# Output projection over 448 instead of 512 rows, with the moved rows placed by DMAs of GpSimd, and two chunks of layer 0 transposed by DMA instead of TensorE

## The chip, the cores and the metric

The kernel runs on one core of a Trainium2 chip. The metric is the device time of one execution in microseconds (us); of several executions the median is taken. Engines are named as the profile names them: PE is TensorE's matmul, PEld its weight load, DVE VectorE, ACT ScalarE, POOL GpSimd, SP the sync engine, whose queue issues most DMAs.

## The reference, cut to what matters

Four layers, alternately A and B, on x of 2048 tokens by 448 values in bfloat16. Layers 0 and 2 are A, layers 1 and 3 are B; both A layers share their weights, and so do both B layers.

```python
def _A_ref(x, wqkv, wo):            # H = 16 heads, Dh = 28, W, dil = 8, 2
    qkv = (x @ wqkv).reshape(B, S, 3, H, Dh).transpose(2, 0, 3, 1, 4)
    q, k, v = qkv[0], qkv[1], qkv[2]
    idx = pos[:, None] - (jnp.arange(W) * dil)[None, :]     # each token: 8 keys, every second one back
    logits = einsum("bhsd,bhswd->bhsw", q, k[idx]) * Dh ** -0.5   # masked where idx < 0
    o = einsum("bhsw,bhswd->bhsd", softmax(logits), v[idx])
    return o.transpose(0, 2, 1, 3).reshape(B, S, D) @ wo    # the output projection
def _B_ref(x, w_gate, w_up, w_down):                        # F = 1792
    return ((x @ w_gate) * (x @ w_up)) @ w_down
x = x + _A_ref(_layernorm(x), A_wqkv, A_wo)
x = x + _B_ref(_layernorm(x), B_w_gate, B_w_up, B_w_down)
x = x + _A_ref(_layernorm(x), A_wqkv, A_wo)
x = x + _B_ref(_layernorm(x), B_w_gate, B_w_up, B_w_down)
```

## The kernel before

**Tokens and layout.** Tokens are reordered: even ones first, odd ones after, so that a key "two back" is a neighbour. They form 16 blocks of 128 tokens. x_sb holds all of x, tokens on partitions. Two neighbouring blocks are a pair; there are 8 pairs in a layer.

**Jobs.** Each layer is cut into chunks of tokens (constants ACH and BCH): layers 0, 1 and 3 into 256, 512, 512, 512 and 256, layer 2 into four of 512. A job is one chunk of one layer. The list SEQ names them in the order in which they are handed to the planner, "A00 A01 B10 A02 ..."; the letter says A or B, then layer and chunk.

**An A job.** ln_chunk normalises each block (bn_stats and bn_aggr on DVE, L630 and L632; logarithm and exponential on ACT, L633 and L635; the product xn_sb on DVE, L651). The normalised block is transposed, to have the features on partitions. That is done by DMA from the sync queue (L654) or, for the chunks in PE_T, by four TensorE transposes (L660) with an eviction by ACT or DVE (L666). In the kernel before, PE_T holds all five chunks of layer 0; layer 2 and the B layers use the DMA. qk_chunk multiplies with the query and key weights (matmuls recorded at L698, evicted at L750), v_group with the value weights (L698, L842). Four of the sixteen heads' values take another way: written to DRAM by the sync queue (vt, L759) and read back by DMA transposes (L770); in layer 0 that holds only from query group 7 on. attn_front computes scores (L862), their exponential (L869) and the mask (L879). attn_back multiplies with the values (L896) and adds (L910, L914).

**Normalisation and projection.** Queries come in groups of 120 tokens (the first has 128), so a pair's columns come from three or four groups. norm spreads the softmax sum over a head's rows (L924), takes its reciprocal through logarithm and exponential (L925, L926), and multiplies into oT (L937, DVE). oT holds the attention output, features on partitions, as [128, 4, 1024]: four chunks c of four heads, each head 28 rows and 4 padding rows, so 4 x 128 = 512 rows of which 448 hold data; 1024 columns of tokens are used as a ring. y_blocks multiplies it with wo_g, the projection weights laid out in the same way with zeros in the padding rows (memset at L529). twin_blocks (matmul at L714) does this for the two blocks of a pair at once: each matmul takes 64 rows, and the upper and lower half of the array work at the same time, in part "flip 0" on one block each, in "flip 1" on the other. Over four chunks that makes 2 parts x 4 chunks x 2 halves = 16 matmuls for a pair. x_block adds the result to x_sb (L954).

**A B job.** b_chunk has 14 units of 14 matmuls for gate and up (L983), a copy by ACT (g_sb, L989), the product on DVE (hT, L992) and the down product (L714 again, or L1004 at the very end), then x_block. In layer 3 the result is stored.

**What sets the order.** The whole program is a list of operations with an estimated duration, dependencies and a priority (lower goes first). Sched.schedule runs through them in its own time and picks for each engine, whenever that is free, the most urgent operation that is ready; what comes out is each engine's fixed order. Priorities are a job's place in SEQ plus the tables JP (by job) and PR (by kind of operation) and HEAD_P for layer 0's normalisation. On PE, gated-product work has mode "R64" (MAIN), and the HOLD constants say when work of other modes goes ahead of it. Sched.emit then writes each engine's instructions in that order, with semaphore waits[...]. The estimates do not run on the chip, they only shape the order.

**Loads.** x is loaded by SP, the first four blocks as two halves; the query and key weights land in stage and are copied into the padded layout WQK by DVE and ACT (L573), with further columns filled in later (L581, by POOL and DVE). wo_g is filled by four DMAs of SP (L500); WD and WGU follow; then one DMA writes the ones into vt.

Of the kernel before, what the change touches and what calls it, by code (L numbers as in the profile page):

```python
# [7 lines left out]
ALU = mybir.AluOpType  # L8
# [20 lines left out]
PE_T = ("00", "01", "02", "03", "04")  # L29
HEAD_LN = 5  # L30
HEAD_P = (-53.71, -30.23, -20.33, -12.94, -19.33)
HOLD_A = 1000.0
HOLD_BA = 2000.0
HOLD_BB = 500.0
HOLD_N = 2
S_EST = 270.0
VX = 120.0
# [3 lines left out]
POOL_WQK = True  # L41
# [10 lines left out]
PR = {'AV': 8.84, 'rstd': -5.66, 'bn': 0.73, 'N': -2.82, 'Gps': -1.08, 'Tps': 16.85, 'H': 18.16, 'S': 10.61, 'VT': 19.61, 'Ex': 16.77, 'G': -2.93, 'xn': -6.19, 'QK': -6.56, 'Ddps': -26.52, 'V': 22.93, 'x': -0.84, 'lnv': -15.5, 'Oc': -6.51, 'Oa': -6.47, 'R': -19.3, 'VVps': 1.22, 'Yps': -25.3, 'PW': 58.69, 'T': -9.57, 'mv': 2.02, 'Rs': -2.57, 'Rl': 21.52, 'QKps': 4.71, 'E': -7.15, 'wqk': -9.31, 'wqp': -11.53}  # L52
JP = {'A20': -3.02, 'B32': 16.28, 'B34': 16.21, 'A22': 20.13, 'B13': 2.73, 'A21': 6.27, 'B12': -2.81, 'A02': -0.21, 'A03': 4.03, 'B30': 4.3, 'B31': 8.23, 'B10': 21.86, 'B11': -14.15, 'A23': 29.86, 'A04': -0.79, 'B33': 153.62, 'A01': -5.33, 'B14': 4.53, 'A00': -24.6}
XL = (2300.0, 2200.0, 4200.0, 5000.0, 5500.0)
WVL = 5000.0
STL = (2400.0, 2600.0, 2900.0, 2800.0)
VONES_L = 18000.0
# [8 lines left out]
SEED = 190  # L66
JITTER = 0
ATT_P = 1.96
# [61 lines left out]
class Sched:  # L130
# [9 lines left out]
    HICCUP = 210.0  # L140

# [5 lines left out]
    def add(self, engs, ins, est, deps=(), prio=0.0, mode=None, acquire=None, release=(), dma=None, lat=0.0, after=None, selfd=(), tmin=None):  # L147
# [8 lines left out]
        for _, k in ins:  # L156
            k = k[0] if isinstance(k, list) and k else k
            if isinstance(k, tuple) and k[0] in PR and k[0] != "cross":
                op.prio += PR[k[0]]
                break  # L160
# [57 lines left out]
    def schedule(self):  # L218
# [6 lines left out]
        credit, clast = self.CREDIT, 0.0  # L225
        ndep, users = {}, {}
# [20 lines left out]
        while left:  # L247
            moved = False
            b_ready = any(o.acquire is not None and o.acquire.kind == 1 for o in pend["pe"])
            for e in self.ENGS:  # L250
# [64 lines left out]
                if e == "pe":  # L315
# [7 lines left out]
                    credit = max(0.0, credit + est / self.FETCH - n)  # L323
                    clast = now + est
# [114 lines left out]
def build(nc, A_x, A_wqkv, A_wo, B_w_gate, B_w_up, B_w_down, out):  # L439
# [24 lines left out]
    wo_g = sb([128, 4, D], bf, "wo_g")  # L464
# [9 lines left out]
    oT = sb([128, 4, HALF], bf, "oT")  # L474
# [11 lines left out]
    sem_names += ["d_x0h"]  # L486
    sem_names += [f"d_t{li}_{j}" for li in range(4) for j in range(len(CH[li]))]
    sem_names += [f"d_p{li}_{j}" for li in (0, 2) for j in range(len(CH[li]))] + [f"d_v{q}" for q in range(NQB)] + ["d_one", "d_stv"]
# [10 lines left out]
    def plain_dma(q, dst, src, key, sem, deps=(), lat=3000.0, prio=0.0, tmin=None):  # L499
# [419 lines left out]
    def norm(li, g, qb, os_, prio):  # L919
# [8 lines left out]
        for B in range(tok // 128, (tok + nq - 1) // 128 + 1):  # L928
            if B >= 8:
                war.append(("Y", li, B - 8))  # L930
            elif li >= 2:
                war.append(("Y", li - 2, B + 8))
# [202 lines left out]
```

## Time and profile before

| | |
|---|---|
| median of 8 runs | 393.54 us (392.35 to 394.4) |
| the profiled execution's own time | 394.22 us |
| its span, from first to last instruction | 392.5 us |
| granted TensorE clock | 1.00 |
| output projection (L714 on wo_g, oT) | 256 matmuls, 349 ns mean of one |
| TensorE transposes (L660) | 64, on layer 0's 16 blocks |
| DMA transposes into xnTa (layer 2) and xnTb (layers 1, 3) | 16 and 32 |
| POOL, busy in all | 7.7 us |

A row of a group gives the line, engine, operation and tiles, then busy time and the mean of one. Matmuls overlap, so a matmul's mean is longer than the spacing of two. A row of a timeline gives start, length, engine and line, and in brackets the idle time before it and what ended it. A row of the table by stage gives the stretch, its length, and each engine's busy time and count, then the clock, the share of the DMA engines and GB/s.

### The profile page before, as it was taken

What the parts mean: (1) busy time and instruction counts of PE and PEld (TensorE: products, weight loads), DVE (VectorE), ACT (ScalarE), POOL (GpSimd) and SP (SyncE); (2) the same over time, 40 slices, a digit from 0 to 9 for tenths busy, and PEclk for the clock granted to TensorE, in tenths of its full rate; (3) what the DMA queues carried; (4) which work ended last, traced back from release to release, by engine and by line L of the source; (5) the groups of instructions that cost most, each with busy time, mean ns of one, the idle gap of its engine ahead of it and who ended that gap; (6) DMA issues with size and microseconds to landing.
All of it is one profiled execution on the core that took longest, in us unless ns stands there. A gap on an engine that the chain in (4) does not pass through costs nothing.

```text
span 392.5 us, 13910 instructions
## 1 busy us (share of the span) xinstructions
PE 384.7 (98%) x6142; PEld 213.8 (54%) x6142; DVE 271.2 (69%) x596; ACT 207.2 (53%) x398; POOL 7.7 (2%) x36
## 2 busy tenths in 40 slices
PE   8989999899999999999999999999999999999997
PEld 6645657545445544554546867444454544544674
DVE  6989899669966865684788645258942689377252
ACT  4888886478523744467651524268315782263230
POOL 6010000000000000000000000000000000000000
PEclk9999999999999999999999999999999999999999
DMA  8990161501220301310120241010050102502101
GB/s 278 294 302 20 24 93 29 107 10 30 48 48 15 78 18 25 69 35 15 17 48 16 42 95 29 25 20 11 8 124 14 26 7 47 97 3 16 34 27 47
DMA packets 54703, 22.47 MB, mean 57 GB/s; under 512 B 44836, under 2 KB 54644, under 8 KB 54644
## 3 DMA queue, kind: packets, MB, share of 16 engines
q1 hardware_dynamic: 53284, 19.47, 23.3%
q10 hardware_dynamic: 1360, 2.12, 1.9%
q8 instruction: 48, 0.79, 0.8%
q14 instruction: 11, 0.09, 0.1%
HBM read 8.54 MB, written 2.71 MB: 29 GB/s over the span
## 4 chain that ended last, share of the span: by engine, by line
PE 91%; DVE 3%; DMA 2%; ACT 2%; issue 1%; DVEq 0%
PE ps L983 41%; PE ps L714 25%; PE ps L698 17%; PE ps L896 3%; PE ps L862 3%; PE ps L1004 1%; DMA xnTb<-xn_sb 1%; PE ps L660 1%; DMA x_sb<-in_A_x_dram 1%; DVE st L630 1%; DVE xn_sb L651 1%; ACT R_sb L925 1%; ACT R_sb L926 1%; DVE x_sb L954 0%; PE ps L565 0%
## 5 line engine op out<-in xcount | busy, mean ns | idle before, releaser
L983 PE MATMUL ps<-xnTb,WGU 64*128 64x512 bf16 (+1 forms) x1960 | 180.5, 333 | 1.0 <-DMA xnTb<-xn_sb 1.0
L983 PEld LDWEIGHTS ps<-xnTb,WGU 64*128 64x128 bf16 x1960 | 93.6, 94 | 73.8 <-ACT g_sb L989 1.5
L989 ACT ACTIVATE g_sb<-ps 128x512 bf16<-128x512 f32 (+1 forms) x140 | 71.4, 510 | 95.2 <-PE ps L983 94.5
L992 DVE TENSOR_TENSOR hT<-g_sb,ps 128x512 bf16<-128x512 bf16 (+1 forms) x140 | 79.4, 575 | 55.3 <-ACT g_sb L989 45.5
L714 PE MATMUL ps<-WD,hT 64*128 64x448 bf16 x840 | 84.0, 349 | 0.1
L714 PEld LDWEIGHTS ps<-WD,hT 64*128 64x128 bf16 x840 | 40.2, 94 | 37.0 <-DVE hT L992 0.7
L698 PE MATMUL ps<-xnTa,WQK 64*128 64x512 bf16 (+1 forms) x504 | 53.5, 353 | 0.2
L954 DVE TENSOR_TENSOR x_sb<-x_sb,ps 128x448 bf16<-128x448 bf16 x62 | 36.2, 615 | 24.9 <-PE ps L714 24.8
L630 DVE BATCH_NORM_STATS2 st<-x_sb 128x6 f32<-128x448 bf16 x64 | 37.5, 617 | 2.5 <-DMA x_sb<-in_A_x_dram 2.5
L869 ACT ACTIVATE E_sb<-ps 128x1024 bf16<-128x1024 f32 (+1 forms) x36 | 33.5, 980 | 10.1 <-PE ps L862 9.5
L750 ACT ACTIVATE qk<-ps 128x1024 bf16<-128x1024 f32 (+1 forms) x30 | 27.1, 921 | 19.3 <-PE ps L698 19.0
L651 DVE TENSOR_SCALAR xn_sb<-x_sb,mv,rstd 128x512 bf16<-128x512 bf16 (+1 forms) x64 | 33.7, 571 | 4.6 <-ACT rstd L635 4.4
L698 PEld LDWEIGHTS ps<-xnTa,WQK 64*128 64x128 bf16 x504 | 23.5, 94 | 23.9 <-ACT xnTa L666 0.8
L879 DVE TENSOR_TENSOR E_sb<-E_sb,MK 128x1024 bf16<-128x1024 bf16 (+2 forms) x40 | 23.9, 613 | 9.2 <-ACT E_sb L869 9.0
L714 PE MATMUL ps<-wo_g,oT 64*128 64x448 bf16 x256 | 29.1, 349 | 0.0
L633 ACT ACTIVATE lnv<-mv,eps_sb 128x2 f32<-128x2 f32 (+1 forms) x33 | 9.5, 293 | 30.3 <-DVE mv L632 30.0
L937 DVE TENSOR_TENSOR oT<-O_sb,R_sb 128x480 bf16<-128x480 f32 (+3 forms) x36 | 22.1, 628 | 3.4 <-ACT R_sb L926 3.1
L925 ACT ACTIVATE R_sb<-R_sb 128x480 f32<-128x480 f32 (+1 forms) x34 | 20.1, 600 | 5.5 <-DVE R_sb L924 5.5
L924 DVE STREAM_SHUFFLE R_sb<-O_sb 128x480 f32<-128x480 f32 (+1 forms) x34 | 22.7, 695 | 0.0
L698 PE MATMUL ps<-WV,xnTa 64*128 64x336 bf16 (+3 forms) x252 | 22.3, 304 | 0.2
L926 ACT ACTIVATE R_sb<-R_sb 128x480 f32<-128x480 f32 (+1 forms) x34 | 20.1, 601 | 0.4
L714 PEld LDWEIGHTS ps<-wo_g,oT 64*128 64x128 bf16 x256 | 12.3, 94 | 11.6 <-DVE oT L937 0.4
(47 smaller groups left out, 170.7 us busy)
## 6 DMA issues: line engine op xcount, KB each, us to landing
out_dram<-x_sb SPq DMA_DIRECT2D x15, 112.0 KB, 1.7
WD<-in_B_w_down_dram SPq DMA_DIRECT2D x2, 784.0 KB, 11.3
WGU<-in_B_w_up_dram SPq DMA_DIRECT2D x2, 784.0 KB, 17.4
WGU<-in_B_w_gate_dram ACTq DMA_DIRECT2D x2, 784.0 KB, 14.1
x_sb<-in_A_x_dram SPq DMA_DIRECT2D x3, 448.0 KB, 6.2
vt<-qk SPq DMA_DIRECT2D x42, 16.0 KB
xnTb<-xn_sb SPq DMA_TRANSPOSE x32, 3.0
x_sb<-in_A_x_dram SPq DMA_DIRECT2D x2, 224.0 KB, 4.0
```

What stands on the lines that cost most here:

```text
L630: sc.add("dve", one(lambda E, B=B: E.bn_stats(st6[:, B, :], x_sb[:, B, :]), ("bn", li, B)), 525.0, deps=[("x", li - 1, B)] + ([("xn", li - ...
L651: sc.add("dve", one(lambda E, B=B, dst=dst, src=src: E.tensor_scalar(dst, src, mv[:, B, 0:1], rstd[:, B:B + 1], ALU.subtract, ALU.mult), ( ...
L698: parts[0 if s < 3 else 1][1].append((lambda E, w=w, c=c, lo=lo, st=st, sp_=sp_: E.matmul(u["out"](w), u["lhs"](w, c, lo, lo + 64), u["rhs ...
L714: ins.append((lambda E, w=w, c=c, lo=lo, st=st, sp_=sp_: E.matmul(outs(w), lhs(w, c, lo), rhs(w, c, lo), start=st, stop=sp_), keys[w] if s ...
L750: return E.activation(dst, src, ACT.Copy) if hasattr(E, "activation") else E.tensor_copy(dst, src)
L869: return E.activation(E_sb[:, slot, 2 * hp:2 * hp + 2, 0:w], ps[:, b0:b0 + 2, 0:w], ACT.Exp, scale=SCALE)
L925: sc.add("act", one(lambda E: E.activation(R_sb[:, rs, 0:w], R_sb[:, rs, 0:w], ACT.Ln), ("Rl", li, qb)), act_est(w, False), deps=[("Rs", l ...
L926: sc.add("act", one(lambda E: E.activation(R_sb[:, rs, 0:w], R_sb[:, rs, 0:w], ACT.Exp, scale=-1.0), ("R", li, qb)), act_est(w, False), de ...
L954: sc.add("dve", one(lambda E: E.tensor_tensor(x_sb[:, B, :], x_sb[:, B, :], ps[:, bk[w], 0:D], ALU.add), ("x", li, B)), dve_est(D), deps=[ ...
L983: ins.append((lambda E, u=u, k=k, w=w: E.matmul(u["out"](w), WGU[64 * w:64 * w + 64, k, 128 * u["fc"]:128 * u["fc"] + 128], X[64 * w:64 * ...
L989: sc.add("act", one(lambda E, gs=gs, bk=bk: E.activation(g_sb[:, gs, 0:nt], ps[:, bk[0], 0:nt], ACT.Copy), ("G", li, j, fc)), act_est(nt), ...
L992: sc.add("dve", one(lambda E, gs=gs, bk=bk, fc=fc: E.tensor_tensor(hT[:, fc, hs, 0:nt], g_sb[:, gs, 0:nt], ps[:, bk[1], 0:nt], ALU.mult), ...
```

## The change

**Projection.** 448 rows are seven halves of 64. For block w = 0 of a pair, the upper half of chunk 3 (heads 14 and 15, 56 rows) is copied into padding rows of the other chunks; for w = 1, the lower half (heads 12 and 13). MOVES lists four copies for each block, of 16, 16, 12 and 12 rows by 128 columns. They are DMAs from oT to oT, issued by POOL in y_blocks after all normalisations that the pair needs. Part flip 0 runs over four chunks as before, flip 1 over three, 14 matmuls for a pair. Both wait for all eight moves. The weights are kept twice, once for each block, with the rows moved in the same way: 16 DMAs of SP in place of four, without the memset, with a later place in SP's order (WO_P). oT becomes a ring of 768 columns, three pairs, that runs on through both A layers.

**Transposes.** Chunks 3 and 4 of layer 0 leave PE_T, so their six blocks are transposed by DMA from SP.

**The rest.** Copies of WQK are assigned by a list, three to ACT and five to DVE, and ACT's also wait for a layer-norm value. The first two blocks of x are loaded by one DMA each, the second by ACT's queue. A gate and up unit waits only for the half of the weights that it reads, and these units keep their order among themselves. The planner gets other priorities, other hold times, other estimates, and a model of instruction fetching on PE (the FL constants, not shown); PR, SEED, ATT_P and STL change too (not shown). SEQ, the number of matmuls in every other product and the tiling stay.

```diff
-PE_T = ("00", "01", "02", "03", "04")
+PE_T = ("00", "01", "02")
...
-HEAD_P = (-53.71, -30.23, -20.33, -12.94, -19.33)
+HEAD_P = (-20.43, -34.51, -10.86, -27.2, -5.58)
...
-POOL_WQK = True
+WQK_ACT = ((0, 0), (0, 1), (2, 0))
...
-JP = {'A20': -3.02, 'B32': 16.28, 'B34': 16.21, 'A22': 20.13, 'B13': 2.73, 'A21': 6.27, 'B12': -2.81, 'A02': -0.21, 'A03': 4.03, 'B30': 4.3, 'B31': 8.23, 'B10': 21.86, 'B11': -14.15, 'A23': 29.86, 'A04': -0.79, 'B33': 153.62, 'A01': -5.33, 'B14': 4.53, 'A00': -24.6}
+JP = {'A23': -110.04, 'B11': -19.53, 'B31': -48.16, 'A21': 10.97, 'A22': -168.43, 'B10': -33.38, 'A00': -17.62, 'B13': -8.8, 'B33': 6.0, 'A04': 7.36, 'A02': 0.78, 'A20': -111.99, 'B30': 1.74, 'B32': 5.39, 'A03': 25.81, 'B34': -31.77, 'A01': -6.89, 'B14': -32.55, 'B12': 1.5}
...
+STL = (2900.0, 3100.0, 3300.0, 3300.0)
+VONES_L = 15000.0
+MVL = 2400.0
+OW = 768
+WO_P = -43.2
+MVE = 1000.0
...
-    wo_g = sb([128, 4, D], bf, "wo_g")
+    wo_g = sb([128, 2, 4, D], bf, "wo_g")
...
-    oT = sb([128, 4, HALF], bf, "oT")
+    oT = sb([128, 4, OW], bf, "oT")
...
+        on_act = (q, lo) == (0, 1)
+        plain_dma("act" if on_act else "sp", x_sb[:, 4 * q + lo:4 * q + hi, :], x_par[two][:, b0 + lo:b0 + hi, :], [("x", -1, B) for B in range(4 * q + lo, 4 * q + hi)],
+                  f"d_x{q}" + "h" * lo, lat=XL[q + (q > 0 or lo > 1)], prio=-62 if on_act else -50 + q + 0.01 * lo)
+
+    load_x(0, 0, 1)
+    load_x(0, 1, 2)
     load_x(0, 2, 4)
...
-    memset("dve", wo_g[:], 0.0, "c_wo", 1000)
...
-            sc.add(("act", "dve", "pool") if POOL_WQK else ("act", "dve"), one(fn, ("wqk", c, w)), {"act": 470.0, "dve": 330.0, "pool": 600.0}, deps=[("stg", c), "c_wqk0"], prio=-28)
+            on_act = (c, w) in WQK_ACT
+            sc.add("act" if on_act else "dve", one(fn, ("wqk", c, w)), 560.0 if on_act else 300.0,
+                   deps=[("stg", c), "c_wqk0"] + ([("rstd", 0, int(WQK_ACT.index((c, w)) >= 1))] if on_act else []), prio=-28)
...
-    plain_dma("sp", ones_dst, ones_src, ("vones",), "d_one", deps=["c_ones"], lat=VONES_L, prio=-40)
-    for j in range(4):
-        dst = wo_g[32 * j:32 * j + DH, :, :]
-        src = A_wo.rearrange("(c j e) d -> j e c d", c=4, j=4, e=DH)[j]
-        plain_dma("sp", dst, src, ("wo", j), "d_wo", deps=["c_wo"], lat=WOL, prio=-45)
+    plain_dma("sp", ones_dst, ones_src, ("vones",), "d_one", deps=["c_ones"], lat=3000.0, est=VONES_L, prio=-40)
+    MOVES = ((0, 0, 64, 16), (0, 32, 96, 16), (0, 64, 80, 12), (0, 96, 112, 12), (1, 64, 0, 16), (1, 96, 32, 16), (1, 0, 16, 12), (1, 32, 48, 12))
+    for j in range(8):
+        src = A_wo.rearrange("(c j e) d -> j e c d", c=4, j=4, e=DH)[j % 4]
+        plain_dma("sp", wo_g[32 * (j % 4):32 * (j % 4) + DH, j // 4, :, :], src, ("wo", j), "d_wo", lat=WOL, prio=WO_P)
+    for n, (w, q, p, k) in enumerate(MOVES):
+        r0 = DH * (12 + p // 32) + p % 32
+        plain_dma("sp", wo_g[q + DH:q + 32, w, 0:k // 4, :], A_wo[r0:r0 + k, :].rearrange("(r c) d -> r c d", r=4), ("wo", 8 + n), "d_wo", lat=WOL, prio=WO_P)
...
-    WO = [("wo", j) for j in range(4)]
+    WO = [("wo", j) for j in range(16)]
...
-        for B in range(tok // 128, (tok + nq - 1) // 128 + 1):
-            if B >= 8:
-                war.append(("Y", li, B - 8))
-            elif li >= 2:
-                war.append(("Y", li - 2, B + 8))
-        cut = [tok] + [HALF] * (tok < HALF < tok + nq) + [tok + nq]
+        g0 = S * (li // 2)
+        for p in range(tok // 256, (tok + nq - 1) // 256 + 1):
+            q = p + 8 * (li // 2) - OW // 256
+            if q >= 0:
+                war += [("Y", 2 * (q // 8), 2 * (q % 8)), ("Y", 2 * (q // 8), 2 * (q % 8) + 1)]
+        cut = [tok] + [t - g0 for t in range(0, 2 * S, OW) if tok < t - g0 < tok + nq] + [tok + nq]
...
-                return E.tensor_tensor(oT[:, :, a % HALF:a % HALF + z - a], O[:, :, a - tok:z - tok], R_sb[:, rs, 0:w].rearrange("p (h n) -> p h n", h=4)[:, :, a - tok:z - tok], ALU.mult)
+                m = (a + g0) % OW
+                return E.tensor_tensor(oT[:, :, m:m + z - a], O[:, :, a - tok:z - tok], R_sb[:, rs, 0:w].rearrange("p (h n) -> p h n", h=4)[:, :, a - tok:z - tok], ALU.mult)
...
-        twin_blocks(lambda w: ps[:, bk[w], 0:D], lambda w, c, lo: oT[lo:lo + 64, c, 128 * ((B + w) % 8):128 * ((B + w) % 8) + 128], lambda w, c, lo: wo_g[lo:lo + 64, c, :],
-                    (("Y", li, B), ("Y", li, B + 1)), [range(4)], [[]], nd + WO, prio, bk)
+        p, m0 = B // 2, (128 * B + S * (li // 2)) % OW
+        for n, (w, q, p0, k) in enumerate(MOVES):
+            dst = oT[q + DH:q + 32, 0:k // 4, m0 + 128 * w:m0 + 128 * w + 128]
+            src = oT[p0:p0 + k, 3, m0 + 128 * w:m0 + 128 * w + 128].unsqueeze(1)
+            sc.add("pool", one(lambda E, dst=dst, src=src: E.dma_start(dst, src), ("OM", li, p) if n == 7 else None), MVE, deps=nd, dma=f"d_m{p}", mode=li, lat=MVL, prio=prio + PR.get("OM", 0.0) * (n < 7))
+        parts = []
+        for flip in (0, 1):
+            ins = []
+            for c in range(4 - flip):
+                for h in (0, 1):
+                    w, lo = h ^ flip, 64 * h
+                    ins.append((lambda E, w=w, c=c, lo=lo, flip=flip: E.matmul(ps[:, bk[w], 0:D], oT[lo:lo + 64, c, m0 + 128 * w:m0 + 128 * w + 128], wo_g[lo:lo + 64, w, c, :],
+                                                                           start=c == 0 and flip == 0, stop=c == 2 and flip == 1),
+                                ("Y", li, B + w) if c == 2 and flip == 1 else None))
+            parts.append((flip, ins, []))
+        crossed(parts, [("OM", li, p)] + WO, prio, pe_cols(D), bk, "Yps")
...
-            return dict(bk=acq, out=out, n=nt, deps=[(w, n) for w in ("wg", "wu") for n in range(2)],
+            return dict(bk=acq, out=out, n=nt, deps=[(w, 128 * fc // (F // 2)) for w in ("wg", "wu")],
...
-            sc.add("pe", ins, 7 * pe_cols(nt), deps=u["deps"] + tdeps, mode=MAIN, prio=prio, acquire=u["bk"])
+            gu_ops.append(sc.add("pe", ins, 7 * pe_cols(nt), deps=u["deps"] + tdeps, mode=MAIN, prio=prio, acquire=u["bk"], after=gu_ops[-1] if gu_ops else None))
```

## The prediction

> **What bounds the kernel now.** I read the page's busy shares first, then the chain that ended last, then the timeline of single engines around the output projection, then a table by stage.
>
> ```profile
> span 392.5 us, 13910 instructions
> PE 384.7 (98%) x6142; PEld 213.8 (54%) x6142; DVE 271.2 (69%) x596; ACT 207.2 (53%) x398; POOL 7.7 (2%) x36
> PE 91%; DVE 3%; DMA 2%; ACT 2%; issue 1%; DVEq 0%
> ```
>
> TensorE is busy for 98% of the span and is 91% of the chain, at full granted clock. So an instruction taken off TensorE is worth its own issue time, as long as nothing else comes late instead. POOL is idle after the start.
>
> The stage table (us from the start; PE, PEld, DVE, ACT busy):
>
> ```profile
> 9.25:39.30 30.05, 28.80 (x615) 16.69 (x616) 27.42 (x74) 24.56 (x52) 1.64 (x6) 1.00 0.75 208
> 57.90:76.00 18.10, 17.04 (x308) 12.02 (x304) 16.42 (x39) 10.80 (x26) 0.00 (x0) 1.00 0.41 59
> 76.00:90.00 14.00, 12.90 (x352) 6.70 (x354) 8.79 (x18) 8.76 (x13) 0.00 (x0) 1.00 0.15 30
> 90.00:200.00 110.00, 110.00 (x1666) 54.34 (x1664) 80.66 (x172) 64.17 (x118) 0.00 (x0) 1.00 0.18 35
> ```
>
> From 90 us on TensorE has no hole worth naming until the tail. Before that it has some: 1.25, 1.06 and 1.10 us in the three stages shown. That is where layer 0's attention must finish so that layer 1's gated product can start, and where VectorE is nearly full as well (27.42 of 30.05 us). A delay can hurt there; later, gated-product work is always at hand to fill it.
>
> How close the output projection follows its input in that early part (timelines of VectorE and TensorE, start and length):
>
> ```profile
> 38.08 0.65 DVE L937 TENSOR_TENSOR oT<-O_sb,R_sb 128x480 bf16<-128x480 f32 x1
> 39.30 0.92 PE L714 MATMUL ps<-wo_g,oT 64*128 64x448 bf16 x8
> 58.53 1.23 DVE L937 TENSOR_TENSOR oT<-O_sb,R_sb 128x480 bf16<-128x480 f32 x2
> 60.18 0.92 PE L714 MATMUL ps<-wo_g,oT 64*128 64x448 bf16 x8
> 76.01 1.69 PE L983 MATMUL ps<-xnTb,WGU 64*128 64x512 bf16 x14 [1.03 <-DMA xnTb<-xn_sb]
> ```
>
> The normalised oT of pair 0 (blocks 0 and 1) is done at 38.73, and its projection starts 0.57 us later; that of pair 2 at 59.76, and its projection 0.42 us later. There is no slack between the two. Layer 1's second chunk (B11, pairs 1 and 2) starts at 76.01 after a wait: residual, layer norm and DMA transpose take 76.01 - 60.18 = 15.8 us from pair 2's projection.
>
> [...] The trace of before has no DMA from GpSimd[...]. Its nearest row is the sync queue's vt<-qk: seven issues in 3.02 us, 0.43 us each. [...]
>
> **The change, part by part.**
>
> *Matmuls removed.* A pair of blocks takes two parts of 8 matmuls; afterwards 8 and 6. Sixteen pairs (8 in each of two layers) lose 2 each, 32 in all. The 349 ns of the row is latency of overlapped matmuls; the rate is on the chain:
>
> ```profile
> 39.46 0.76 PE ps L714 x8
> 13.15 1.00 PE ps L660 x16
> ```
>
> 0.76 / 8 = 95 ns each, so 32 x 95 = 3.0 us, all on TensorE.
>
> *Transposes removed.* Layer 0's chunks 3 and 4 are six blocks, 24 TensorE transposes. At 1.00 / 16 = 62.5 ns that is 1.5 us; their four bursts on TensorE's timeline last, from start to the next start, 0.62 (at 23.69), 0.33, 0.55 and 0.33, 1.83 us with the changes of mode. I take 1.8. Their evictions go as well: three on ScalarE of 605 ns, three on VectorE of 422 ns, in the stage in which VectorE is fullest. I count no time for that.
>
> *Transposes added.* Six DMA transposes at 1.3 us each are 7.8 us of the sync queue, landing 2.5 us after issue (layer 2's own). The sync queue issues its loads until 17.7 us and then nothing until 39.09. The output weights now take 16 issues instead of 4: 12 x 0.48 (four in 1.93 us) = 5.8 us, so loads end at about 23.5 us, and the transposes fit before the vt writes queued behind them. In the kernel before, chunk 4's product starts at 38.85 and chunk 3's at about 46, so the longer landing is hidden. Cost zero; if the queue were blocked, a few us of delay would meet the early holes, which the rivals price.
>
> *Moves added.* Per pair eight GpSimd DMAs, 128 in all. Issue: at least 0.43 us (sync queue's row)[...]; I take 1.0. Landing after the last issue: 1.5 to 2.5 us from the rows of small and transposing DMAs here; I take 2.0. So oT is ready 8 x 1.0 + 2.0 = 10 us after the normalisation[...]. They use no TensorE time, and 128 us of an idle POOL. Behind the waiting move on POOL stand only later moves (the pad copies of WQK are over by 25.6). From 90 us on, the 10 us lie beside gated-product work, provided the attention chunks run that much earlier; the diff gives layer 2's chunks much more urgent priorities (A22 from +20 to -168, A23 from +30 to -110). Pair 7 of layer 2 is the tightest: normalised at 352.04, used at 366.94; but its q/k product was done by 301, so its attention has room to move up.
>
> In the early part I walk it through. Pair 2 with normalisation unmoved at 59.8: moves until 67.8, landed 69.8, so 9.6 us later than 60.18, and B11 is ready at 85.6. TensorE work that lies after 76 in the kernel before and needs nothing of B11: scores and value products at 77.62, 82.71, 84.94 and 87.03 (0.7, 0.7, 0.7, 1.3), two down products of 1.43, value projections at 90 of 2.0: 8.3 us. So 9.6 - 8.3 = 1.3 us of new idle. Moving chunks 3 and 4 behind the earlier attention shortens that; A03's priority becomes less urgent in the diff. I take 0.8 us.
>
> *Small parts.* Ring oT of 768 columns: a normalisation waits for the projection three pairs back instead of four; pair 3's needs pair 0's, about 49 us against 59. Zero; if it waited, VectorE's hT products behind it would be late. Three more splits at ring edges: (388 + 418 - 655) ns each, 0.5 us of VectorE, hidden. The oT weights' memset (0.8 us of VectorE at 1.2 us) goes, in idle time. WQK copies: five on VectorE and three on ScalarE instead of four each; the first x block loaded separately. Together between -0.6 and +0.6 us at the first product (9.25); I take 0. Order constants of the plan: no time of their own.
>
> *Sum.* -3.0 - 1.8 + 0.8 = -4.0 us. The profiled execution took 394.22 (span 392.5 and 1.7 around it), giving 390.2. It lies 0.7 above the median of the eight runs, 393.54; from that, 389.5. This is the forecast, with its own range of 388.0 to 391.6.
>
> **Rivals.**
> 1. *The slower side: GpSimd's issue rate.* Pairs 0, 1 and 2 queue on POOL from 38.7 on. At t us a move, pair 2 has landed no earlier than 38.7 + 24 t + 2. At 1.5 that is 76.7, 16.5 us later than before; less 8.3 us of cover, 8.2 us idle: 393.5 - 4.8 + 8.2 = 396.9. Idle equals the gain at 13.1 us late, t = 1.36: from there it decides. For it: sixteen separate rows per move[...]. Against: POOL has nothing else to do[...].
> 2. *The gain is spent early.* The moves are fast enough, but the early order isn't changed enough, or the new DMA transposes come behind the output weights and the ones on the sync queue; 4 us instead of 0.8 idle: 392.7. For it: VectorE is nearly full there, so attention can't be pulled forward freely.
> 3. *More than the sum.* The six evictions gone and the earlier x load remove 1.0 of the 1.25 us of holes before 39.3 and 0.6 at the start, without new idle: 393.5 - 4.8 - 1.6 = 387.1. For it: VectorE's 27.42 of 30.05 us.
> 4. That 448 rows don't remove two matmuls per pair can be excluded from the diff: flip 1 runs over three chunks.
>
> **How the numbers follow.** Forecast 0.58, more 0.13, spent early 0.10 (half of it within 0.2%, half faster), slower 0.19. A measurement of this kernel tells about 0.2% (0.8 us) from no change. Faster 0.58 + 0.13 + 0.05 = 0.76; same 0.05; slower 0.19. The range leaves out the lower part of "more" and about half of rival 1: 386.6 to 395.5.
>
> **What would show it.** 224 projection matmuls instead of 256 and 40 transposes instead of 64; TensorE's busy time down by about 4.8 us; POOL with 128 issues spaced about 1 us; some 10 us from oT's normalisation to its projection, with no TensorE hole behind it after 90 us. I am wrong if moves are spaced over 1.36 us, if L983's first 512-column product starts after about 86 us with more than 4 us of new idle before it, or if TensorE waits for moves late in layer 2.

## The result, and the profile after

The kernel after takes 398.01 us (median of 11 runs, 395.95 to 403.61), the kernel before 393.39 us beside it (32 runs). One run of after, 403.61 us, fell in a slower state that some executions show, and the ratio leaves it out: 1.0128, with a 95% interval of 1.0107 to 1.0149. By the medians the change costs 4.6 us where 4.0 us less were forecast, a gap of 8.6 us. The profiled execution of after took 395.95 us and is the fastest of its runs.

The page of the kernel after, busy shares and chain:

```profile
span 394.2 us, 13936 instructions
PE 382.5 (97%) x6086; PEld 218.3 (55%) x6086; DVE 273.7 (69%) x598; ACT 201.6 (51%) x390; POOL 81.1 (21%) x166
PE 92%; ACT 3%; DMA 1%; DVE 1%; issue 1%; SPq 0%
```

TensorE has 56 matmul records fewer, as expected (32 of the projection, 24 transposes). Yet it is busy for only 2.2 us less, and idle for 394.2 - 382.5 = 11.7 us instead of 392.5 - 384.7 = 7.8. So 3.9 more idle less 2.2 less work make the 1.7 us by which this span is longer.

Where, by stage. Kernel after, the four stages that the prediction showed (stretch, length, PE, PEld, DVE, ACT, POOL busy, clock, DMA share, GB/s):

```profile
9.25:39.30 30.05, 25.16 (x492) 13.70 (x494) 22.20 (x63) 24.57 (x49) 2.09 (x8) 0.94 1.08 243
57.90:76.00 18.10, 17.00 (x365) 13.59 (x361) 15.13 (x34) 10.98 (x22) 7.73 (x14) 1.00 0.42 71
76.00:90.00 14.00, 13.95 (x280) 8.40 (x276) 13.23 (x33) 8.39 (x20) 0.00 (x0) 1.00 0.52 66
90.00:200.00 110.00, 110.00 (x1654) 54.24 (x1650) 80.08 (x163) 56.81 (x104) 22.74 (x40) 1.00 0.24 38
```

The first row holds the loss: 4.89 us idle where it was 1.25, a granted clock of 0.94 where it was 1.00, and DMA engines that are full to the end (1.08; before 0.75). In the third row the change even gains: 0.05 us idle, before 1.10. From 9 to 64 us TensorE is idle 7.1 us (before 1.4), from 64 to 90 us 1.0 (before 2.2).

TensorE's timeline in the kernel after (start, length, line, tiles, count, then idle time before it and what ended it):

```profile
26.23 0.89 PE L885 MATMUL ps<-qk 28*64 28x64 bf16 x71 [1.12 <-issue]
28.51 3.89 PE L721 MATMUL ps<-xnTa,WQK 64*128 64x512 bf16 x20 [1.38 <-ACT E_sb L892]
32.33 0.51 PE L919 MATMUL ps<-E_sb,v_sb 64*32 64x64 bf16 x36
34.84 0.30 PE L919 MATMUL ps<-E_sb,v_sb 64*32 64x64 bf16 x28 [2.00 <-issue]
```

The hole that ends at 34.84 stands in the middle of one group of 64 matmuls, 36 before it and 28 after it. Nothing they read was missing: "issue" means that no semaphore explains the wait. What was missing, by my reading, were instructions: the profile names the kind of one DMA queue, q8, "instruction", and it carries 48 packets of 16 KB in a run. Each is called a refill here. A row of the next tables gives a DMA queue, its packets, MB, and share of the DMA engines. Queues of the kernel before from 28.5 to 30.5 us:

```profile
q1 hardware_dynamic: 459, 0.25, 57.3%
q10 hardware_dynamic: 18, 0.03, 5.6%
q8 instruction: 1, 0.02, 4.2%
```

and of the kernel after, first from 28 to 31.9 us, then from 31.9 to 33.4 us:

```profile
q1 hardware_dynamic: 670, 0.54, 63.3%
q10 hardware_dynamic: 216, 0.36, 41.6%
```

```profile
q1 hardware_dynamic: 683, 0.31, 138.6%
q8 instruction: 1, 0.02, 5.2%
```

In the kernel before the third refill starts at 28.84, when q10 (the gate weights) has all but ended. In the kernel after it starts at 32.00 and ends at 33.24; TensorE goes on 1.6 us later. Counted in the trace, TensorE stops after its 961st record (matmuls, weight loads and semaphore instructions); it stops at that same count in each kernel below that has this hole, whatever its order. The 1.12 us hole that ends at 26.23 stands after record 705, 256 earlier, and ends 1.6 us after the second refill; in the kernel before, a hole of 0.41 us stands there, and it too ends 1.6 us after the second refill. TensorE's 12,314 records in the run of after, on 48 packets, are 257 to a packet, close to the 256 between the two stops. The reading rests on these counts and times; the trace names no wait for instructions.

Behind such holes the clock can fall. Kernel after, in steps of 2 us:

```profile
28.00:30.00 2.00, 1.40 (x10) 0.46 (x12) 1.56 (x3) 2.00 (x3) 0.00 (x0) 0.91 1.06 216
30.00:32.00 2.00, 2.00 (x12) 0.62 (x8) 1.48 (x3) 1.19 (x2) 0.00 (x0) 0.50 1.08 250
32.00:34.00 2.00, 0.84 (x38) 0.38 (x37) 0.00 (x0) 1.02 (x1) 0.00 (x0) 0.73 1.65 175
```

The clock record gives half speed for 3.41 us from 29.65, so 1.7 us of work is lost; in a run's mean clock that is 0.004. This window follows the holes of 1.12 and 1.38 us; the 2.00 us hole begins as it ends, and no window follows that one in this run. The runs of after show 0.996 to 0.983, one to four such windows, and are in the main the longer the lower it is (395.95 and 396.54 us at 0.996; 400.05 and 401.63 at 0.983). The profiled run of before shows 1.00, with holes of 1.03 and 1.09 us (ending at 76.00 and 88.65 us) and no window. Windows follow holes of 1 to 3 us in these runs (1.12 and 1.38 us here, 2.67 us in f3 below); how long a hole must be for one to follow is not shown.

Why the refill is late: it waits among the weights. It does not wait for their end: the second refill starts amid them in both kernels (23.10 us before, 23.54 after), and in two experiments below, f4 and g2, the third starts at 32.6 and 32.5 us while the up weights fill the DMA engines until 38. What grows is the wait. No record says when a refill is asked for, so I count from record 706, the first behind the place that lies 256 records earlier: the third refill starts 3.0 us later in the kernel before and 5.8 us later in the kernel after. What differs between the two is how the weights load. Issues of the kernel before, then of the kernel after (KB each, median us from issue to landing where the profile has it):

```profile
WGU<-in_B_w_up_dram SPq DMA_DIRECT2D x2, 784.0 KB, 17.4
WGU<-in_B_w_gate_dram ACTq DMA_DIRECT2D x2, 784.0 KB, 14.1
...
wo_g<-in_A_wo_dram SPq DMA_DIRECT2D x4, 98.0 KB
```

```profile
WGU<-in_B_w_up_dram SPq DMA_DIRECT2D x2, 784.0 KB, 15.7
WGU<-in_B_w_gate_dram ACTq DMA_DIRECT2D x2, 784.0 KB, 17.9
...
wo_g<-in_A_wo_dram SPq DMA_DIRECT2D x8, 98.0 KB
...
wo_g<-in_A_wo_dram SPq DMA_DIRECT2D x4, 14.0 KB
wo_g<-in_A_wo_dram SPq DMA_DIRECT2D x4, 10.5 KB
```

The output weights grow from four loads of 98 KB to sixteen, 490 KB more, and stand behind the other weights that the sync queue loads. The up weights (partitions 64 to 127) land earlier, the gate weights (partitions 0 to 63) 3.8 us later: they no longer run side by side. Up weights alone, kernel after:

```profile
17.00:19.50 2.50, 2.50 (x56) 1.12 (x52) 2.50 (x11) 2.33 (x7) 0.00 (x0) 1.00 1.07 175
```

and both together, kernel before:

```profile
20.00:28.00 8.00, 7.00 (x128) 3.51 (x127) 6.63 (x18) 6.17 (x10) 1.64 (x6) 1.00 1.06 323
```

175 GB/s against 323, with DMA engines that look equally full. That one queue was at work instead of two is not the reason: from 12 to 15 us of the kernel after the sync queue alone moved 343 GB/s, loading the down weights into all 128 partitions. So the load into 64 partitions alone moved half of what the load into 128 did, and the two halves side by side, at 323 GB/s, 1.8 times as much as one alone. What makes one half slow is not shown.

### The profile page after: what moved, and what is told of

The parts are those of the page before. It is cut to its first block, busy times and chain, and to the rows that moved or that the text cites. A ratio compares the mean times of both kernels' runs of the same rounds, so it can differ in the third digit from the quotient of the medians.

```text
span 394.2 us, 13936 instructions
## 1 busy us (share of the span) xinstructions
PE 382.5 (97%) x6086; PEld 218.3 (55%) x6086; DVE 273.7 (69%) x598; ACT 201.6 (51%) x390; POOL 81.1 (21%) x166
## 4 chain that ended last, share of the span: by engine, by line
PE 92%; ACT 3%; DMA 1%; DVE 1%; issue 1%; SPq 0%
PE ps L1022 43%; PE ps L737 20%; PE ps L721 17%; PE ps L983 5%; PE ps L885 2%; PE ps L919 2%; DMA x_sb<-in_A_x_dram 1%; PE ps L1043 1%; ACT E_sb L892 1%; ACT qk L773 1%; ACT xnTa L689 0%; SPq L517 0%; PE ps L683 0%; ACT R_sb L948 0%; DVE E_sb L902 0%
## 5 line engine op out<-in xcount | busy, mean ns | idle before, releaser
L1022 PEld LDWEIGHTS ps<-xnTb,WGU 64*128 64x128 bf16 x1960 | 96.4, 94 | 69.6 <-issue 1.3
L976 POOL DMA_DIRECT2D oT<-oT x128 | 72.9, 576 | 229.6 <-DVE oT L961 205.0
L1031 DVE TENSOR_TENSOR hT<-g_sb,ps 128x512 bf16<-128x512 bf16 (+1 forms) x140 | 79.6, 576 | 35.5 <-ACT g_sb L1028 30.5
L737 PEld LDWEIGHTS ps<-WD,hT 64*128 64x128 bf16 x840 | 42.0, 94 | 37.0 <-issue 0.6
L721 PE MATMUL ps<-xnTa,WQK 64*128 64x512 bf16 (+1 forms) x504 | 54.4, 359 | 2.5 <-ACT E_sb L892 1.4
L653 DVE BATCH_NORM_STATS2 st<-x_sb 128x6 f32<-128x448 bf16 x64 | 37.5, 614 | 3.8 <-DMA x_sb<-in_A_x_dram 3.7
L721 PEld LDWEIGHTS ps<-xnTa,WQK 64*128 64x128 bf16 x504 | 24.8, 95 | 25.1 <-ACT E_sb L892 2.3
L773 ACT ACTIVATE qk<-ps 128x1024 bf16<-128x1024 f32 (+1 forms) x28 | 25.6, 919 | 15.6 <-PE ps L721 15.3
L983 PE MATMUL ps<-wo_g,oT 64*128 64x448 bf16 x224 | 26.3, 349 | 0.5 <-ACT E_sb L892 0.5
L961 DVE TENSOR_TENSOR oT<-O_sb,R_sb 128x480 bf16<-128x480 f32 (+11 forms) x39 | 22.0, 590 | 5.9 <-ACT R_sb L949 5.4
L948 ACT ACTIVATE R_sb<-R_sb 128x480 f32<-128x480 f32 (+1 forms) x34 | 19.7, 603 | 3.1 <-DVE R_sb L947 3.1
L949 ACT ACTIVATE R_sb<-R_sb 128x480 f32<-128x480 f32 (+1 forms) x34 | 19.6, 600 | 0.2
```

The costliest lines, as they stand in the source:

```text
L653: sc.add("dve", one(lambda E, B=B: E.bn_stats(st6[:, B, :], x_sb[:, B, :]), ("bn", li, B)), 525.0, deps=[("x", li - 1, B)] + ([("xn", li - ...
L721: parts[0 if s < 3 else 1][1].append((lambda E, w=w, c=c, lo=lo, st=st, sp_=sp_: E.matmul(u["out"](w), u["lhs"](w, c, lo, lo + 64), u["rhs ...
L737: ins.append((lambda E, w=w, c=c, lo=lo, st=st, sp_=sp_: E.matmul(outs(w), lhs(w, c, lo), rhs(w, c, lo), start=st, stop=sp_), keys[w] if s ...
L773: return E.activation(dst, src, ACT.Copy) if hasattr(E, "activation") else E.tensor_copy(dst, src)
L976: sc.add("pool", one(lambda E, dst=dst, src=src: E.dma_start(dst, src), ("OM", li, p) if n == 7 else None), MVE, deps=nd, dma=f"d_m{p}", m ...
L983: ins.append((lambda E, w=w, c=c, lo=lo, flip=flip: E.matmul(ps[:, bk[w], 0:D], oT[lo:lo + 64, c, m0 + 128 * w:m0 + 128 * w + 128], wo_g[l ...
```

## The experiments

Each kernel was timed beside the kernel before (393.2 to 393.9 us in each batch). The expectations name their guesses by letters: A, the order at the start and late refills; B, the moves; C, the late DMA transposes; D, the projection's part; C2 and C3, the weight loads; E, something else. Where they say that a refill lands at 28.8 or 32.0 us, that is its start. The order of an engine is planned, and a planner that gets other durations or dependencies plans everything anew. Therefore most experiments keep every engine's order and edit single places in it; where a plan had to be made anew, this is said.

**e1: the moves away** (order of after kept; the moves are gone from POOL and the projection waits for the normalisation alone, so the padding rows hold old values).

```diff
-  pool: all 128 moves oT<-oT
-  projection waits for ("OM", layer, pair)
+  projection waits for the normalisations of its pair
```

> The changed kernel with every engine's order kept, but the 128 moves of GpSimd left out: the projection waits for the normalisation alone. It leaves out the moved rows, so the padding rows of oT hold softmax sums. Theory A (the loss sits in the first 64 us and comes from the order at the start, from a crowded DMA stage with late instruction refills, and from the halved TensorE clock that follows the holes): the moves cost nothing worth naming, so 397 to 399 us, as the changed kernel's 398.0. Theory B (the moves' 5 to 10 us between normalisation and projection are what came late): 4 us or more faster, 394 or less.

396.46 us, ratio 1.0066 [1.0043, 1.0089]. Neither theory's range is met. Set against after's 1.0128 the moves, with the wait for them, cost 2.4 us in this order (1.2 to 3.7 us, from the two intervals). So they are a part of the loss, but without them the kernel is still 2.6 us slower than before, with 3.0 us of matmuls fewer. How they cost it is not shown: in the profiled run of after TensorE waits for no move, and the profile of e1 is of its longest run (401.07 us).

**e2, e3 and e4: start and place of the output weights** (order of after kept; e2 restores the order of VectorE and ScalarE in the first 12 us; e3 puts the 16 output weight loads behind the first five transposes of the sync queue; e4 is both).

```diff
 e2 dve: ("mv",0,1) right behind ("bn",0,1); four WQK copies behind ("xn",0,3)
 e3 sp:  ("wo",0..15) behind ("T",0,14)
```

> The changed kernel; only the order of the first 12 us on VectorE and ScalarE is mended: the statistics of block 4, which wait for the second load of x, go behind the normalised blocks 1 to 3 and the last three weight copies, and the layer norm of block 1 goes ahead of ScalarE's other work. Theory A: the first q/k product moves from 11.9 back to between 9.3 and 10.2, and the time falls by 1.5 to 2.6 us, to about 396. Theory B: no change, 398.

> The changed kernel; only the 16 loads of the output weights are moved on the sync queue, behind the first five DMA transposes of layer 0. Theory A: the DMA engines are less crowded from 20 to 35 us, the refill that TensorE waits for at 33 comes about 2 us earlier, most of the 3.1 us of issue holes go and with them the half-clock windows; 3 to 5 us faster, 393 to 395. Theory B: no change, or a little slower since the writes to vt come later: 398 to 399.

> Both edits of the two kernels before: the order of the start and the later loads of the output weights. Theory A: the two gains add up, 390.5 to 392.5, below the kernel before the change. Theory B: 398.

e2 398.66 us, ratio 1.0127 [1.0102, 1.0151]: no gain, the value product still waits for its weights until 10.46. e3 400.99, ratio 1.0196 [1.0164, 1.0228], e4 399.79, ratio 1.0158 [1.0138, 1.0178]: no gain either, e3 slower. Neither edit mends the loss. In e3 the transposes run amid the other weights and the third refill starts at 33.94 instead of 32.00.

**e5 to e8: one part of the change alone** (e5, e6 and e8 planned anew; e7 keeps the order of before).

```diff
 e5 after:   -PE_T = ("00", "01", "02")   +PE_T = ("00", "01", "02", "03", "04")
 e6 before:  -PE_T = ("00", "01", "02", "03", "04")   +PE_T = ("00", "01", "02")
 e7 before:  +six times, behind ("vones",) on sp, from ("S", 0, 2) on:
             +E.dma_start_transpose(xnT[1][:, 0:4, 128*i:128*i+128], wo_g[..][:, 0:512])
 e8 after:   e5, and the x loads and WQK copies of before
```

> The kernel after, but all layer 0 blocks are transposed on TensorE again (24 transposes added in four-block bursts, six DMA transposes gone); the planner's priorities had to be searched anew for it, so the order of the first 60 us differs too. Projection on 448 rows and moves by GpSimd stay. Theory C (the six DMA transposes stand in the time in which the weights load, delay TensorE's instruction refills, and the holes of 1 to 2 us between 25 and 36 us that follow halve the clock): granted clock 1.00, holes of 25 to 37 us under 1.5 us in sum, 390 to 392 us. Rival D (the cause is the projection's part: 16 weight loads instead of 4, moves, the start of the first products): clock below 1 again, 396 to 399 us.

> The kernel before with one part of the change alone: layer 0 blocks 10 to 15 transposed by DMA (six DMA transposes on the sync queue, 24 TensorE transposes gone), priorities searched anew for it; projection on 512 rows, moves in the sync queue's old form. Theory C: holes at 25 to 37 us, granted clock 0.99 or lower, 395 to 399 us. Rival D (the late transposes are harmless, the projection's part is at fault): 24 transposes saved, 391.5 to 393 us, clock 1.00.

> The kernel before, its order on every engine untouched, with six DMA transposes of the same shape (128 rows to 128x4x128) added on the sync queue from about 25 us on; they read the output weights and write a part of a buffer that is not yet in use, so nobody waits for their data until layer 1 (after 60 us). Nothing is left out. It measures what the six transposes cost by their mere presence: shared DMA engines, the sync queue, and the instruction refills. Theory C: 0.5 to 4 us more than before (394 to 397.5), TensorE holes named issue at 26 to 37 us larger than the 1.0 us of before, the refill that landed at 28.8 us in before landing 2 us or more later. Rival D: 393.5, same as before, refill within 0.5 us of before.

> The other part of the change alone: projection on 448 rows, 16 weight loads, moves by GpSimd as in the kernel after; all layer 0 blocks transposed on TensorE, first x loads and copies of the q/k weights as in the kernel before, priorities searched anew. Theory C: clock 1.00, 3.0 us of matmuls gained, 390 to 392 us. Rival D: 396 to 399 us, with holes at 25 to 37 us and a clock below 1.

e5 397.15 (ratio 1.0087 [1.0059, 1.0116]), e6 399.2 (1.0138 [1.0109, 1.0166]), e7 393.69 (1.0001 [0.9983, 1.0018]), e8 397.5 us (1.0098 [1.0063, 1.0133]). e7 refutes theory C in its general form: six DMA transposes from 25.9 us on cost nothing, and the third refill starts at 28.91. e8 has no late DMA transposes and still its third refill starts at 32.30, with a hole of 2.56 us. So the lateness comes with the projection's part, and not by the moves, the first of which is issued at 41.0 us in the kernel after. A late refill is not the only loss, though: e5's starts at 33.01, but TensorE comes to record 961 only at 37.03 and has no hole there; its longest waits are 1.44 us at record 705 and 2.11 us for a masked exponential.

e6 shows something else, on the sync queue (min, median and max ns of one issue; who waited; landing):

```profile
L654 SPq DMA_TRANSPOSE xnTa<-xn_sb x22: 1190/1267/7251, 20.9 to 240.7; - x22
...
  PE ps L698: 5.5, 1
...
DMA to landing us min/median/max: 2.4/2.5/11.3
```

The first transpose, issued at 20.9 us amid the weights, held the queue for 7.25 us and landed after 11.3, and TensorE waited 5.5 us for it. In e7, from 25.9 us on, the same six took at most 3.2 us each and nobody waited. So in e6 late transposes do harm, because somebody needs them while the weights load.

**f1 to f4: the weight loads alone** (every engine's order kept, apart from the loads on the sync queue).

```diff
 f1 after:   ("wu",0), ("wu",1) behind ("wo",15)
 f2 before:  ("wo",0..3) behind ("wu",1)
 f3 before:  f2, and twelve more loads there: 4 x 98 KB, 4 x 14 KB, 4 x 10.5 KB
             +plain_dma("sp", flat[q+DH:q+32, ...], A_wo[r0:r0+k, :]...)   # into xnTb, nobody reads
 f4 before:  the sixteen loads of f3 in the place of the four
```

> The kernel after, every engine's order kept, but on the sync queue the two loads of the up weights (partitions 64 to 127) stand behind the 16 loads of the output weights instead of ahead of them, so that they run together with the gate weights (partitions 0 to 63, Scalar queue). Theory C2 (in the kernel after the up weights run alone from 16 to 20 us and the gate weights alone from 26 to 31 us, at about 150 ns a packet instead of 80; the weights are in 3 us later, TensorE's third instruction refill waits for that, lands at 32.0 instead of 28.8 us, and TensorE stands still until 1.6 us after it; a half-clock window follows): third refill before 30.5 us, the 2.0 us hole that ends at 34.84 us gone, clock 0.995 or better, 394 to 396.5 us. Rival E (the refill is late for another reason in this order): refill at 32 us as before the edit, 397 to 399 us.

> The kernel before, every engine's order kept, but its four loads of the output weights stand behind the down and up weights on the sync queue, as in the kernel after. Theory C2: the up weights start about 1.3 us earlier than the gate weights and end earlier, so the gate weights run alone for some 1 to 2 us; third refill at 29 to 30.5 us, 393.5 to 395 us. Rival E: refill at 28.8 us and 393.5 us as before.

> The kernel before, every engine's order kept, with the weight loads of the kernel after: 16 loads on the sync queue behind the down and up weights (the four that it has, and twelve more of the same sizes and patterns as the kernel after has, into a part of a buffer that is not used before layer 1; nobody reads them). Nothing else of the change is in it. Theory C2: third refill at 31 to 32.5 us, a hole of 1.5 to 2.5 us behind it, one to three half-clock windows, 396 to 399 us. Rival E: 393.5 to 394.5 us, third refill within 0.7 us of 28.8.

> As f3, the same 16 loads, but ahead of the down and up weights, where the kernel before has its four. Theory C2 (place decides): up and gate weights end together, third refill at 29 to 30.5 us, 393.5 to 395.5 us. Rival (number and bytes decide, not the place): as f3, third refill at 31 to 32.5 us, 396 to 399 us.

f1 399.92 us (ratio 1.0144 [1.0121, 1.0167]), f2 395.71 (1.0052 [1.003, 1.0074]), f3 397.48 (1.0093 [1.007, 1.0115]), f4 398.5 (1.0127 [1.0097, 1.0157]). f3 shows what the loads do by themselves: the kernel before, with the loads of after and nothing else of the change, loses 3.7 us. TensorE of f3:

```profile
31.54 0.20 PE L908 MATMUL ps<-E_sb,v_sb 64*32 64x64 bf16 x3
34.42 0.66 PE L908 MATMUL ps<-E_sb,v_sb 64*32 64x64 bf16 x61 [2.67 <-issue]
```

and its clock behind that hole:

```profile
34.00:36.00 2.00, 1.58 (x71) 1.11 (x73) 0.84 (x2) 0.85 (x2) 0.00 (x0) 0.91 0.23 54
36.00:38.00 2.00, 2.00 (x12) 0.75 (x10) 2.00 (x8) 0.79 (x2) 0.00 (x0) 0.50 0.00 0
```

The same place in the kernel before, without a hole:

```profile
29.63 2.15 PE L698 MATMUL ps<-xnTa,WQK 64*128 64x512 bf16 x16
31.71 0.68 PE L896 MATMUL ps<-E_sb,v_sb 64*32 64x64 bf16 x64
```

2.67 us of hole and 1.7 of half clock are 4.4; the spans of the two profiled runs differ by 3.3, so 1.1 is made up later. f2, the place alone without added bytes, makes most of the lateness and half of the loss: refill at 31.44, hole 2.11, 1.9 us. The rest is in the windows: five of f2's twelve runs have one or more, five of f3's six. f2's runs also show the price of one window: seven with a clock of 1.00 have a median of 394.78 us, five with 0.996 one of 397.25. f4 and f1 were expected to mend it and did not. In f4 the sixteen loads ahead hold back the up weights: the gate weights run without them until 29 us, and they then run alone until 38 us (150 ns a packet; 81 and 82 where both halves run, from 24 to 28 us of the kernel before). The third refill starts at 32.62. In f1 the gate weights run first and the up weights behind them: second refill at 26.29, third at 35.30, and holes of 3.94 and 3.17 us. So a swap does not restore the two halves side by side. That they must run together, with the added loads out of the way, was read from these two misses; g1 and g2 test it.

**g1 to g3: the projection's part with mended loads** (448 rows and moves as in after, all layer 0 transposes on TensorE, first x loads and WQK copies as in before; the order of before up to 38 us in g1 and g2, 32 us in g3, the rest planned anew).

```diff
 g1, g3 sp:  ("wo",0..3) where before has its four; ("wo",4..15) behind ("vones",)
             +("wo",4) waits for ("AV", 0, 2), a TensorE group at 32 us
 g2 sp:      ("wo",0..15) where before has its four
```

> Projection on 448 rows with the moves by GpSimd, all layer 0 blocks transposed on TensorE; the order of the first 38 us is that of the kernel before on every engine, the rest is planned anew. The first four output weight loads stand where the kernel before has its four, the other twelve wait on the sync queue until a TensorE instruction at about 32 us is done. Theory C3 (the twelve added loads delay the refills, the rest of the change does what the prediction's sum says): third refill at 28.5 to 29.5 us, no hole over 1 us at 31 to 36 us, granted clock 1.00, 393.7 less 3.0 for the matmuls: 390 to 391.5 us. Rival (moves and new order eat the gain): 393 to 396 us with clock 1.00.

> As g1, but all 16 output weight loads at one place, ahead of the down and up weights; nothing else differs. Theory C3: third refill at 31.5 to 33 us, a hole of 2 to 3 us at about 33 to 36 us, clock 0.996 or lower, 4 to 5 us more than g1: 394 to 396.5 us. Rival: within 1.5 us of g1.

> As g1, with another planned order from 32 us on (another search of the priorities). Theory C3: 390 to 392 us, clock 1.00; it shows how much of g1's time is the order's luck. Rival: 393 to 397 us.

g1 395.09 us (22 runs, 392.85 to 398.59; ratio 1.0054 [1.0037, 1.0072]), g2 400.32 (1.0204 [1.0173, 1.0236]), g3 396.58 (1.0077 [1.0046, 1.0108]). g1 and g2 differ in the place of twelve loads and nothing else, by 5.2 us. g1's third refill starts at 29.34, and where g2 has a hole of 2.66 us g1 has none. That half of the expectation held. The profile of g2 has, besides, one half-clock window more, a hole of 1.10 us at record 705, and a wait of 1.70 us for a move that ends at 90.16. The other half did not hold: g1 should have been at 390 to 391.5. Its timeline:

```profile
31.88 0.68 PE L922 MATMUL ps<-E_sb,v_sb 64*32 64x64 bf16 x64
...
41.74 0.71 PE L888 MATMUL ps<-qk 28*64 28x64 bf16 x64 [0.22 <-ACT v_sb L868]
44.62 1.89 PE L724 MATMUL ps<-xnTa,WQK 64*128 64x512 bf16 x8 [2.17 <-ACT E_sb L895]
```

There is a new hole of 2.17 us, this time a product that waits for an exponential, and a half-clock window that begins in it. Why the plan has it there is not shown. Twenty of its 22 runs have at least one window (0.996 or less); the two without took 392.85 and 393.02. From 393.16 for before, less 3.0 for the matmuls, plus 2.2 for this hole: 392.4. These two runs fit a projection that gains its 3.0 us, with a hole and its window eating it; they are too few to show it. In g3 it is a 2.8 us wait for a transpose of layer 1. No version that was timed beats the kernel before. A plan of g1 without its hole should come to about 390.8 (393.0 - 2.2), which is an estimate from these numbers; three further plans of that kind (h1 to h3, expected at 389 to 391.5 us) were written and not timed.

## Why the prediction was wrong

**What held.** 32 projection matmuls fewer at 95 ns: the chain of after has 0.76 us for 8 and 0.57 for 6. 40 transposes instead of 64. The delay from normalisation to projection is hidden after 90 us: no TensorE hole from there to the tail. The move's landing (2.0 predicted, 1.8 measured). The issue was set at 1.0 us and took 0.58 (0.74 at most). The 1.0 was an assumption: the kernel before has no DMA from GpSimd, only the sync queue's 0.43 us, and its trace gives no upper bound. So eight moves and a landing are about 6.4 us and not 10, and rival 1 (from 1.36 us a move) is out. The row of the moves:

```profile
L976 POOL DMA_DIRECT2D oT<-oT x128 | 72.9, 576 | 229.6 <-DVE oT L961 205.0
```

**The step that failed** is the one headed "Transposes added": "The output weights now take 16 issues instead of 4: 12 x 0.48 (four in 1.93 us) = 5.8 us, so loads end at about 23.5 us, and the transposes fit before the vt writes queued behind them. [...] Cost zero". It priced twelve loads as time of the queue that issues them, and at nothing for what they move and for their place behind the other weights. Measured, the sixteen issues run from 13.4 to 26.7 us while the DMA engines are full (a share of 1.08). Their data and their place part the two halves of the weights and keep the loads coming until about 32 us instead of 28.5; the third instruction refill waits 5.8 us instead of 3.0; TensorE stands, and loses clock. f3 puts 3.7 us on the loads alone in the order of before, g1 and g2 put 5.2 us on their place in another order, out of the 8.6 us between forecast and result. The rest of the gap is not shown by any experiment to be the loads'.

**Terms of the sum.** Idle time added early was set at 0.8 us, for a wait of B11 for the moves, and none came: from 64 to 90 us TensorE is idle 1.1 us less than before. The idle time came earlier, 5.7 us more from 9 to 64 us, for other reasons. Of it, 2.0 us are the hole of the third refill and 0.7 us what the second refill's hole grew by (1.12 instead of 0.41). Another 3.1 us are waits that the order of after has and that of before has not: 1.38 us for the exponential, then 0.88, 0.46 and 0.34 us between 48 and 53 us. At the start, 0.5 us before the second transposes stands against a wait of 0.6 us for a WQK column in the order of before. Half clock was in no term: 1.7 us in the profiled run and more in most others. In that run, +5.7 - 1.1 + 1.7 - 4.8 = 1.5 us, against 1.7 between the spans.

**Small parts** were set at nothing, +-0.6, at the first q/k product. It came at 11.89 instead of 9.25, though the value product starts at 10.20 and fills part of it. e2 did not settle which part of the new start costs what.

**The rivals.** Rival 2 named the place (early, behind the output weights) and not the mechanism: it expected transposes to be late, while TensorE, as read here, ran out of instructions. Its 4 us of idle lies near the 3.9 more that the page shows; that is luck, for the idle time has other causes. The sign that the prediction gave for its own failure (first 512-column product after 86 us with over 4 us of new idle before it) half came: it starts at 87.80, but with 0.94 us of idle ahead of it since 64 us, and is no loss.

**What stays open.** What the six late DMA transposes cost in the kernel after itself: e5 (without them, order planned anew) is 0.9 us faster than after, which is within what another order makes. How the moves come to cost 1.2 to 3.7 us (e1), and what the waits of the order of after cost each: no experiment has that order with the loads mended. What a refill waits behind in the DMA engines: the wait is longer where packets take longer (before: 3.0 us, with gate packets of 81 ns from 24 to 28 us; after: 5.8 us, with 129 ns from 28 to 31.9 us), but no run tests how. And whether the projection's 3.0 us can be kept in a finished plan: g1 and g3 show that orders of the same work differ by 1.5 us.

## What to carry to other kernels

Price an added load in three currencies: the time of its issue, the time for which it keeps the DMA engines full, and what else waits for these engines. Here instruction refills are among that: the third waited 5.8 us instead of 3.0, and a hole of 2.00 us named "issue" stood in the middle of a group. In this kernel, loads that go to one half of the partitions should run beside loads to the other half (323 GB/s against 175), and the added output weights should wait until the others are in, as in g1 (5.2 us faster than g2). Count the clock with a hole: in f3 a hole of 2.67 us was followed by half clock that cost 1.7 us more. And a gain of 3 us is easily lost in a new plan: g1's order has a wait of its own, of 2.17 us.

## What the runs showed of the hardware

- The third refill, in us. The wait is counted from record 706 to the refill's start. In the first group both halves of the weights load side by side, in the second one half loads alone for most of the wait, in the third DMA transposes stand among the weights as well:

| kernel | wait | start | hole after record 961 |
|---|---|---|---|
| before | 3.0 | 28.84 | none |
| e6 | 2.6 | 28.57 | none |
| e7 | 3.4 | 28.91 | none |
| g1 | 3.3 | 29.34 | none |
| g3 | 3.8 | 29.44 | 0.47 |
| f2 | 5.6 | 31.44 | 2.11 |
| f3 | 6.2 | 31.88 | 2.67 |
| after | 5.8 | 32.00 | 2.00 |
| e1 | 5.3 | 35.70 | 2.83 |
| e2 | 5.7 | 32.08 | 1.10 |
| e8 | 6.0 | 32.30 | 2.56 |
| g2 | 5.7 | 32.48 | 2.66 |
| f4 | 5.7 | 32.62 | 2.39 |
| e5 | 6.0 | 33.01 | none, TensorE itself was late |
| f1 | 6.0 | 35.30 | 3.17 |
| e3 | 7.9 | 33.94 | 3.62 |
| e4 | 8.6 | 34.95 | 4.31 |

- In the holes of 1 us and more TensorE goes on 1.3 to 1.6 us after the refill's end. With the DMA engines nearly idle (a share of 0.04 from 37.5 to 39 us; fifth refill of before, 37.98 us) the wait, counted from record 1218, is 0.05 us, and no hole follows; in all kernels that wait lies between -0.7 and 1.0 us.
- A packet of 1792 bytes of the up or gate weights took, in the median of a stretch, 81 to 102 ns where both halves load (before, 20 to 24 us: 102 up and 101 gate; 24 to 28: 82 and 81; after, 20 to 24: 82 and 85). Up weights alone took 172 ns (after, 17 to 19.5 us), gate weights beside the output weights 141 ns (after, 26 to 31 us).
- Loads in GB/s: 175 for the up weights alone (64 partitions; after, 17 to 19.5 us), 323 for up and gate weights together (before, 20 to 28 us), 343 for the down weights alone (128 partitions; after, 12 to 15 us).
- Half clock lasted 3.41 us in the profiled run of after, from 29.65 us, behind holes of 1.12 and 1.38 us.
- Matmuls of 64 rows start in pairs: in a projection of before, at 39.30 us, the two of a pair 3 ns apart and the pairs 189 ns apart, 95 ns a matmul, while one takes 349 ns. TensorE's transposes start 56 ns apart; the matmul that follows them starts 152 ns after the last (before, 32.66 us).
- A move of 12 or 16 rows by GpSimd takes 576 ns to issue (mean; 570 to 742) and lands after 1.7 to 1.8 us (medians).
- A DMA transpose issued into full DMA engines (e6, at 20.9 us) held its queue for 7.25 us and landed after 11.3; the median of that kernel's 22 is 1.27 and 2.5 us. In the kernel after the first late transpose held it for 5.24 us, from 27.61 us, and the next issue of the sync queue started 0.05 us behind its end.
